# The last seven value steps as 64-row tiles in two PSUM banks, two of them set between score pairs

## The chip, the core and the metric

The kernel runs on one core of one Trainium2 chip. The metric is device time in microseconds (us), the median of repeated runs. Before the change it is 1230.41 us (three runs, 1230.26 to 1230.48). Durations and waits come from one profiled execution of the kernel before; its span from first to last instruction is 1229.5 us.

## The reference: attention with one key head, a gated FFN, and a gate that mixes them

```python
def _A_ref(x, wq, wk, wv, wo):                    # S = 2048, D = 512, H = 32, Dh = 16
    q = (x @ wq).reshape(B, S, H, Dh).transpose(0, 2, 1, 3)
    k = x @ wk                                    # one key and one value head for all 32
    v = x @ wv
    scores = einsum("bhqd,bkd->bhqk", q, k) * (Dh ** -0.5)
    p = softmax(scores, axis=-1)
    o = einsum("bhqk,bkd->bhqd", p, v)
    return o.transpose(0, 2, 1, 3).reshape(B, S, H * Dh) @ wo

def _B_ref(x, w_gate, w_up, w_down):              # F = 1376
    return (gelu(x @ w_gate) * (x @ w_up)) @ w_down

g = sigmoid((x * gate_w).sum(-1, keepdims=True))
return g * _A_ref(x, ...) + (1 - g) * _B_ref(x, ...)
```

All inputs are 32-bit floats.

## The kernel before

**The two kinds of attention step.** Scores are made transposed, keys on the partitions. One *score pair* (S in the plan, `scores`, line 745) is two matmuls of 51 rows by 128 columns over 512 queries, one per head, one in the lower and one in the upper 64 rows of TensorE's array. They fill a tile `s` of 128x1024 (two PSUM banks), and ScalarE takes one exponential over it into `p` (line 749). A *value visit* (V in the plan, `pv`, line 816) multiplies the `p` of four heads by the values: four matmuls of 128 rows (128 keys) by 32 columns, head j writing partitions 32j to 32j+31 of `acc`, one PSUM bank. Data is plain 32-bit there, and each such matmul appears in the trace as two, so a visit is eight. Two score pairs feed one visit. A unit `u` is four heads by 512 queries over 16 key chunks, so 16 visits; there are 32 units and 512 visits.

**The FFN in between.** Gate, up and down projections run as pairs of matmuls `z` and `y` (`pair_mm`, line 515), each 64 rows by 128 columns, in the two row halves of the array at once. `z` lies in one of the three `s` tiles, `y` in the bank of pool `ps_f`. PSUM has eight banks: three `s` tiles of two, one for `acc` (`ps_a`), one for `y` (`ps_f`).

**What sets the order.** The table `PLAN` is the order of TensorE's work written out by hand, one line for each FFN job, with letters that `play` carries out: H starts a job, F is one pair of its matmuls, R ends it and puts its evictions on VectorE, S is a score pair, Z a score pair into the third `s` tile, V2 is two visits. Engines work their own queues in that order. The last line is the last down projection, and then the last seven visits (505 to 511) with the last four score pairs.

**What comes after the last visit.** `norm(31)` is the last normalisation: on VectorE, in two halves of 256 columns, it forms the denominators (`zsum`, line 776) and numerators (`nsum`, line 779) straight from `acc`, then line 773 (a shuffle), 782 (reciprocals), 785 (the product), 790 and 794 (the split in a high and a low part, `oh` and `ol`). For the other units `acc` is copied to a tile `n1` first. Meanwhile TensorE makes the output projection of the last 512 queries, 36 matmuls for three of four head blocks in the tiles `wos` (three) and `wof` (in `ps_f`), and then 12 matmuls with the block that `norm` has just finished; VectorE adds each of the four results to `acc` of the FFN (line 627), and SP's queue writes it out (line 628).

Of the kernel before, what the change touches and what calls it, by code (L numbers as in the profile page):

```python
# [9 lines left out]
F32 = mybir.dt.float32  # L10
# [9 lines left out]
P = 128  # L20
S = 2048
D = 512
H = 32
DH = 16
F = 1376
TG = 512
NTG = S // TG
NC = D // P
NKC = S // P
# [12 lines left out]
EVERY = 3  # L42
PB = 12
STAGE = 4
PLAN = [
# [62 lines left out]
]  # L108


# [1 line left out]
def mix_kernel(ctx, tc, xT, wq, wo, wf, out):  # L112
    nc = tc.nc
# [4 lines left out]
    ps_f = ctx.enter_context(tc.tile_pool(name="ps_f", bufs=1, space=PSUM))  # L118
# [73 lines left out]
    vt = pp.tile([P, TG], F32, name="vt")  # L192
# [122 lines left out]
    def source(kind, n, c):  # L315
        if kind == "x":
            return xT[n, :, c]
        if kind == "o":
            return wo[:, c]
        t = 2 if kind == "d" else c  # L320
        return wf[(chunks[n][1] - 1) % NF][:, t * D : (t + 1) * D]
# [23 lines left out]
    def fetch():  # L345
        while supply and len(raw) < STAGE - 1:
            p = supply.pop(0)
            t = cp.tile([P, D], F32, tag="st", name="st", bufs=STAGE)
            nc.sync.dma_start(t, source(*p))
            raw.append((p, t))  # L350
# [86 lines left out]
    for ti, tg in enumerate(order):  # L437
        xh, xl = xs[tg]
        last = ti == NTG - 1
# [55 lines left out]
    def flush(q):  # L495
        while q:
            q.pop(0)()
# [144 lines left out]
    def ffn_jobs():  # L642
        for n, (tg, r) in enumerate(chunks):
            if r and n > 1:
                yield gate_job(n)
            if r == 5 or r == NF - 1:
                flush(chain)
                batch = hold[:]
                hold.clear()
                if r == NF - 1 and tg + 1 < NTG:  # L650
                    reload_h(tg + 1)
                for i in (0, 2):
                    yield down_job(batch, i)

    def wo_jobs():
        for g in range(NTG - 1):
            for i in (0, 2):
                yield wo_job(g, i)

    nsteps = 8 * NTG * NKC  # L660
# [24 lines left out]
    with tc.If(v > 0):  # L685
        with tc.tile_pool(name="gp", bufs=1) as gp:
# [4 lines left out]
            with tc.For_i(0, NTG * NB, 1) as gb:  # L691
                with tc.For_i(0, 2, 1) as a:
# [4 lines left out]
                    for i in range(4):  # L697
                        for h in range(4):
                            rs = slice(64 * (h % 2), 64 * (h % 2) + KR)
# [27 lines left out]
    pb = {}  # L727
    accp = {}
# [22 lines left out]
    def norm(u):  # L751
        g, ub = divmod(u, 8)
        b, a = divmod(ub, 2)
        ac = accp.pop(u)
        new = lambda tag: mp.tile([P, TG], F32, tag=tag, name=f"{tag}{u}", bufs=1)
        if a == 0:
            flush(bg)
            c0, tz = new("n0"), new("nz")
            nc.vector.tensor_copy(c0, ac)
            bg.append(lambda: nc.vector.tensor_scalar(tz, c0, mkb, None, op0=ALU.mult))  # L760
            bg.append(lambda: nc.vector.tensor_scalar(c0, c0, mk, None, op0=ALU.mult))
            at[g, b] = c0, tz
            return
        N, z = at.pop((g, b))
        last = u == 8 * NTG - 1
        r = new("n1")
        c1 = ac
        if not last:
            c1 = r
            nc.vector.tensor_copy(c1, ac)  # L770

        def shuffle(cs):
            nc.vector.stream_shuffle(r[:, cs], z[:, cs], [(i + 16) % 32 for i in range(32)])

        def zsum(cs):
            nc.vector.scalar_tensor_tensor(z[:, cs], c1[:, cs], mk, z[:, cs], op0=ALU.mult, op1=ALU.add)

        def nsum(cs):
            nc.vector.scalar_tensor_tensor(N[:, cs], c1[:, cs], mkb, N[:, cs], op0=ALU.mult, op1=ALU.add)

        def recip(cs):
            nc.vector.reciprocal(z[:, cs], r[:, cs])

        def scale(cs):
            nc.vector.tensor_mul(N[:, cs], N[:, cs], z[:, cs])

        def high(cs):
            if (g, b) not in O:
                O[g, b] = [mp.tile([P, TG], F32R, tag=t, name=f"{t}{u}", bufs=4) for t in ("oh", "ol")]
            nc.vector.tensor_copy(O[g, b][0][:, cs], N[:, cs])  # L790

        def low(cs):
            oh, ol = O[g, b]
            nc.vector.tensor_sub(ol[:, cs], N[:, cs], oh[:, cs])

        if last:
            flush(bg)
            for cs in (slice(0, 256), slice(256, 512)):
                for fn in (zsum, nsum, shuffle, recip, scale, high, low):
                    fn(cs)  # L800
            return
        full = slice(0, TG)
        for fn in (zsum, nsum, shuffle):
            bg.append(lambda fn=fn: fn(full))
        for i in range(4):
            bg.append(lambda i=i: recip(slice(i * P, (i + 1) * P)))
        for fn in (scale, high, low):
            bg.append(lambda fn=fn: fn(full))

    def pv(s):  # L810
        u, kc = divmod(s, NKC)
        if kc == 0:
            accp[u] = ps_a.tile([P, TG], F32, tag="pa", name=f"acc{u}")
        vt = (v1, v2)[u % 2]
        for j in range(4):
            nc.tensor.matmul(accp[u][32 * j : 32 * j + 32], vt[:, kc], pb[s][:, j // 2, (j % 2) * TG : (j % 2 + 1) * TG],  # L816
                             start=(kc == 0), stop=(kc == NKC - 1), skip_group_check=True)
        del pb[s]

    at_s, at_v = [0], [0]  # L820
# [5 lines left out]
    def visit(k):  # L826
        flush(chain if at_v[0] == 0 else [])
        for _ in range(k):
            assert 2 * at_v[0] + 1 < at_s[0]
            pv(at_v[0])  # L830
            at_v[0] += 1
            if at_v[0] % NKC == 0 and at_v[0] < nsteps:
                norm(at_v[0] // NKC - 1)
# [37 lines left out]
    queues = {"f": ffn_jobs(), "w": wo_jobs()}  # L871
    for line in PLAN:
        kind, word = line.split(":")
# [4 lines left out]
    now[0] += 16  # L878
    run_later()
    norm(8 * NTG - 1)  # L880

    g = NTG - 1
# [49 lines left out]
```

## Time and profile before

| | |
|---|---|
| median of the runs | 1230.41 us (1230.26 to 1230.48) |
| profiled execution, first to last instruction | 1229.5 us |
| PE busy | 1222.6 us (99%) |
| ACT busy | 1029.4 us (84%) |
| DVE busy | 546.1 us (44%) |
| POOL busy | 216.9 us (18%) |
| granted TensorE clock, mean | 0.999 |

The runs' median lies 0.9 us above the profiled span. PE is TensorE's matmuls, PEld its weight loads, DVE is VectorE, ACT ScalarE, POOL GpSimd. A busy PE counts from a matmul's start to its modelled end, and matmuls overlap; so how fast PE goes is read from the distance of starts. In a row of the timeline the first two numbers are the start and the stretch that the merged instructions cover, and the bracket at the end is the idle time before them on that engine, and what ended it.

### The profile page before, as it was taken

To read this page: it belongs to the slowest core of one execution; us is meant where nothing else is said; L and a number is where in the kernel's file an instruction comes from. 1 tells how busy PE (TensorE), PEld (TensorE's weight loads), DVE (VectorE), ACT (ScalarE), POOL (GpSimd) and SP (SyncE) were. 2 spreads that over 40 slices of the span, in tenths; PEclk is the share of its full clock that TensorE was granted. 3 is DMA by queue.
4 is the path that set the end of the run, shared out by engine and by line. 5 is a ranking of instruction groups with operands and counts; after the bars stand their busy time and mean duration, and the time that the engine had idled before them with its cause. 6 is when DMAs were issued, how large, how long until landed. Compare 5 with 4: busy or idle time off the path is not lost.

```text
span 1229.5 us, 23232 instructions
## 1 busy us (share of the span) xinstructions
PE 1222.6 (99%) x9742; PEld 671.4 (55%) x9742; DVE 546.1 (44%) x812; ACT 1029.4 (84%) x1127; POOL 216.9 (18%) x188
## 2 busy tenths in 40 slices
PE   9999999999999999999999999999999999999998
PEld 6875455555554555455555555654554555545545
DVE  7774422656245151545436152263626244044624
ACT  5549888888888888998888888889888898889983
POOL 5422201222121010212112020121311011012100
PEclk9999999999999999999999999999999999999999
DMA  8641202212021110122211120111211211002000
GB/s 333 211 135 52 72 1 58 66 53 79 27 68 51 44 32 23 49 57 67 66 35 58 39 76 15 42 44 56 83 41 49 75 49 32 23 27 66 15 1 35
DMA packets 39835, 73.88 MB, mean 60 GB/s; under 512 B 5488, under 2 KB 5744, under 8 KB 39728
## 3 DMA queue, kind: packets, MB, share of 16 engines
q1 hardware_dynamic: 39184, 71.32, 18.9%
q8 instruction: 77, 1.26, 0.4%
q0 software_dynamic: 256, 0.79, 0.2%
q14 instruction: 30, 0.25, 0.1%
q10 hardware_dynamic: 288, 0.26, 0.1%
HBM read 57.41 MB, written 14.94 MB: 59 GB/s over the span
## 4 chain that ended last, share of the span: by engine, by line
PE 93%; DVE 0%; ACT 0%; issue 0%
PE acc L816 38%; PE s L745 23%; PE z L515 21%; PE y L515 10%; PE wos L501 1%; PE u L501 0%; DVE acc L627 0%; ACT p L749 0%; PE wof L501 0%; DVE sq L545 0%; DVE sq L544 0%; DVE gs L541 0%; ACT sq L548 0%
## 5 line engine op out<-in xcount | busy, mean ns | idle before, releaser
L749 ACT ACTIVATE p<-s 128x1024 f32<-128x1024 f32 x1024 | 976.3, 1026 | 139.1 <-PE s L745 136.2
L816 PE MATMUL acc<-p,v 128*32 128x512 f32 x4096 | 484.8, 597 | 0.0
L745 PE MATMUL s<-Q,kp 51*128 51x512 f32 x2048 | 384.8, 415 | 0.1
L745 PEld LDWEIGHTS s<-Q,kp 51*128 51x128 f32 x2048 | 184.2, 184 | 214.1 <-ACT p L749 124.0
L816 PEld LDWEIGHTS acc<-p,v 128*32 128x32 f32 x4096 | 114.3, 109 | 250.8 <-issue 242.1
L187 POOL TENSOR_TENSOR gl<-st,gh 128x512 fp32r<-128x512 f32 x80 | 114.0, 1444 | 754.3 <-PE s L745 375.5
L515 PE MATMUL z<-xh,gh 64*128 64x512 f32 x312 | 125.9, 403 | 0.0
L515 PE MATMUL y<-xh,gh 64*128 64x512 f32 x312 | 125.8, 403 | 0.0
L515 PE MATMUL y<-xl,gh 64*128 64x512 f32 x312 | 122.4, 392 | 0.0
L515 PE MATMUL z<-xl,gh 64*128 64x512 f32 x312 | 122.1, 391 | 0.0
L515 PE MATMUL z<-xh,gl 64*128 64x512 f32 x312 | 121.8, 390 | 0.0
L515 PE MATMUL y<-xh,gl 64*128 64x512 f32 x312 | 121.7, 390 | 0.0
L541 DVE COPY gs<-z 128x512 f32<-128x512 f32 x39 | 27.0, 692 | 195.3 <-PE y L515 128.5
L187 POOL TENSOR_TENSOR dl<-st,dh 128x512 fp32r<-128x512 f32 x44 | 57.3, 1304 | 127.8 <-PE s L745 94.0
L515 PE MATMUL z<-dh,hh 64*128 64x512 f32 x176 | 69.5, 395 | 0.0
L515 PE MATMUL y<-dh,hh 64*128 64x512 f32 x176 | 69.5, 395 | 0.0
L515 PE MATMUL y<-dl,hh 64*128 64x512 f32 x176 | 68.9, 392 | 0.0
L515 PE MATMUL z<-dl,hh 64*128 64x512 f32 x176 | 68.8, 391 | 0.0
L515 PE MATMUL z<-dh,hl 64*128 64x512 f32 x176 | 68.8, 391 | 0.0
L515 PE MATMUL y<-dh,hl 64*128 64x512 f32 x176 | 68.7, 391 | 0.0
L515 PEld LDWEIGHTS z<-xh,gh 64*128 64x128 f32 x312 | 58.0, 186 | 15.6 <-POOLq L523 7.3
L515 PEld LDWEIGHTS z<-xl,gh 64*128 64x128 f32 x312 | 58.3, 187 | 8.2
(173 smaller groups left out, 1458.0 us busy)
## 6 DMA issues: line engine op xcount, KB each, us to landing
st<-wf SPq DMA_DIRECT2D x125, 256.0 KB
scr<-q SPq DMA_DIRECT2D x16, 512.0 KB
Q<-scr SPq DMA_DIRECT2D x64, 128.0 KB
Q<-scr SPq DMA_DIRECT2D x64, 64.0 KB
out<-acc SPq DMA_DIRECT2D x16, 256.0 KB
xr<-xT SPq DMA_DIRECT2D x6, 512.0 KB
st<-xT SPq DMA_DIRECT2D x12, 256.0 KB
xr<-xT SPq DMA_DIRECT2D x4, 256.0 KB
```

The source lines that it names most:

```text
L187: eng_l.tensor_sub(lo, src, hi)
L501: nc.tensor.matmul(ps, a, b, start=(first and q == 0), stop=(last and q == len(terms) - 1), skip_group_check=True)
L515: mm = nc.tensor.matmul(ps, a[rs], b[rs], start=(half == 0 and q == 0), stop=(half == 1 and q == len(X) - 1), skip_group_check=True)
L541: nc.vector.tensor_copy(gs, g)
L745: nc.tensor.matmul(ps[:, j * TG : (j + 1) * TG], kp[rs, kc * P : (kc + 1) * P], Q[u][rs, pr], start=True, stop=True)
L749: nc.scalar.activation(pb[s][:, pr], ps, AF.Exp, bias=0.0, scale=SCALE)
L816: nc.tensor.matmul(accp[u][32 * j : 32 * j + 32], vt[:, kc], pb[s][:, j // 2, (j % 2) * TG : (j % 2 + 1) * TG], start=(kc == 0), stop=(kc ...
```

## The change

The last seven visits are each eight matmuls in place of four: the 128 keys are split in two halves of 64 rows, and the tile is 64 rows by 32 columns. The lower half adds on to `acc`; the upper half goes to a second PSUM bank, `accb`, which begins with the first of the seven. `accb` is taken from the pool `ps_f`, the bank in which `y` of the last down projection lies. The last normalisation first copies `acc` to a tile in SBUF, adds `accb` to it, and goes on from that tile. In the last line of the plan the seven visits stand as one, one and five, not as two and five.

```diff
+HALVES = 7
 PLAN = [
...
-    "f: H F S F5 S F3 S F6 S2 F6 S F3 S F3 S F3 R S V2 S2 Z V5",
+    "f: H F S F5 S F3 S F6 S2 F6 S F3 S F3 S F3 R S V S V S Z V5",
 ]
...
         r = new("n1")
-        c1 = ac
-        if not last:
-            c1 = r
-            nc.vector.tensor_copy(c1, ac)
+        c1 = r
+        nc.vector.tensor_copy(r, ac)
...
         if last:
             flush(bg)
+            nc.vector.tensor_add(r, r, accp.pop((u, 1)))
             for cs in (slice(0, 256), slice(256, 512)):
                 for fn in (zsum, nsum, shuffle, recip, scale, high, low):
                     fn(cs)
...
         vt = (v1, v2)[u % 2]
+        by_halves = nsteps - s <= HALVES
+        if nsteps - s == HALVES:
+            accp[u, 1] = ps_f.tile([P, TG], F32, tag="pf", name="accb")
         for j in range(4):
-            nc.tensor.matmul(accp[u][32 * j : 32 * j + 32], vt[:, kc], pb[s][:, j // 2, (j % 2) * TG : (j % 2 + 1) * TG],
-                             start=(kc == 0), stop=(kc == NKC - 1), skip_group_check=True)
+            cols = slice(32 * j, 32 * j + 32)
+            w = pb[s][:, j // 2, (j % 2) * TG : (j % 2 + 1) * TG]
+            if by_halves:
+                for r, ac in ((0, accp[u]), (64, accp[u, 1])):
+                    rs = slice(r, r + 64)
+                    nc.tensor.matmul(ac[cols], vt[rs, kc], w[rs], start=(r > 0 and nsteps - s == HALVES),
+                                     stop=(kc == NKC - 1), skip_group_check=True)
+            else:
+                nc.tensor.matmul(accp[u][cols], vt[:, kc], w, start=(kc == 0), stop=(kc == NKC - 1), skip_group_check=True)
         del pb[s]
```

First, TensorE's order at the last visits, from the score pair after the last FFN matmul to the five visits at the end, before (`Q`, `kp` are the queries and keys, `v_76` the values; a wait names the engine that is waited for):

```order
L745 MATMUL s<-Q_12177,kp 128x512 [waits Activation_49]
L745 MATMUL s<-Q_12177,kp 128x512
L816 MATMUL acc_12577<-p,v_76 32x512 x8
L745 MATMUL s<-Q_12177,kp 128x512 [waits Activation_49]
L745 MATMUL s<-Q_12177,kp 128x512
L745 MATMUL s<-Q_12177,kp 128x512 [waits Activation_49]
L745 MATMUL s<-Q_12177,kp 128x512
L745 MATMUL s<-Q_12177,kp 128x512 [waits DVE_49]
L745 MATMUL s<-Q_12177,kp 128x512
L816 MATMUL acc_12577<-p,v_76 32x512 x14
```

The same place in the change, its first score pair, first visit and the pair behind it:

```order
L746 MATMUL s<-Q_12177,kp 128x512 [waits Activation_49]
L746 MATMUL s<-Q_12177,kp 128x512
L824 MATMUL acc_12577<-p,v_76 32x512
L824 MATMUL accb<-p,v_76 32x512 [waits DVE_49]
L824 MATMUL acc_12577<-p,v_76 32x512
L824 MATMUL accb<-p,v_76 32x512
L824 MATMUL acc_12577<-p,v_76 32x512
L824 MATMUL accb<-p,v_76 32x512
L824 MATMUL acc_12577<-p,v_76 32x512
L824 MATMUL accb<-p,v_76 32x512
L746 MATMUL s<-Q_12177,kp 128x512 [waits Activation_49]
L746 MATMUL s<-Q_12177,kp 128x512
```

A score pair has moved up between the first and the second visit, and the second matmul of the first visit waits for VectorE, which no visit there did before.

Second, VectorE's order from the last evictions of the down projection to the first steps of the last normalisation, before:

```order
L617 SCALAR_TENSOR_TENSOR acc_11092<-y,gc,acc_11092 128x512 [waits PE_49]
L776 SCALAR_TENSOR_TENSOR nz_12513<-acc_12577,mk,nz_12513 128x256 [waits PE_49]
L779 SCALAR_TENSOR_TENSOR n_12512<-acc_12577,mkb,n_12512 128x256 [waits DVE_49]
L773 STREAM_SHUFFLE n_12851<-nz_12513 128x256 [waits DVE_49]
L782 RECIPROCAL nz_12513<-n_12851 128x256 [waits DVE_49]
```

And in the change:

```order
L618 SCALAR_TENSOR_TENSOR acc_11092<-y,gc,acc_11092 128x512 [waits PE_49]
L769 COPY n_12880<-acc_12577 128x512 [waits PE_49]
L797 TENSOR_TENSOR n_12880<-n_12880,accb 128x512 [waits DVE_49,PE_49]
L775 SCALAR_TENSOR_TENSOR nz_12513<-n_12880,mk,nz_12513 128x256 [waits DVE_49]
L778 SCALAR_TENSOR_TENSOR n_12512<-n_12880,mkb,n_12512 128x256
L772 STREAM_SHUFFLE n_12880<-nz_12513 128x256 [waits DVE_49]
L781 RECIPROCAL nz_12513<-n_12880 128x256 [waits DVE_49]
```

Two instructions over all 512 columns stand ahead of the first half; everything behind them has kept its order. Elsewhere no engine's order differs.

## The prediction

> **What bounds the kernel now.** I read the page's busy times first, then the chain of waits, then the timeline of the last 25 us, where everything that is changed lies.
>
> ```profile
> PE 1222.6 (99%) x9742; PEld 671.4 (55%) x9742; DVE 546.1 (44%) x812; ACT 1029.4 (84%) x1127; POOL 216.9 (18%) x188
> PE 93%; DVE 0%; ACT 0%; issue 0%
> ```
>
> TensorE sets the end: 93% of the chain is PE. So a change costs what it adds to PE's path, plus what it adds behind PE's last matmul. The chain in order of time, near its end:
>
> ```profile
> 1189.98 2.71 PE acc L816 x24
> 1192.70 0.89 PE s L745 x6
> 1193.59 3.57 PE acc L816 x32
> 1197.16 0.43 PE s L745 x2
> ...
> 1205.48 0.23 PE s L745 x2
> ...
> 1206.40 0.24 PE s L745 x2
> 1206.64 1.85 PE acc L816 x16
> 1208.49 0.89 PE s L745 x6
> 1209.39 4.43 PE acc L816 x40
> 1213.82 6.34 PE wos L501 x27
> 1220.16 2.04 PE wof L501 x9
> 1222.20 0.69 PE wos L501 x3
> 1222.90 0.02 issue
> 1222.92 2.79 DVE acc L627 x4
> ```
>
> Prices come out of these rows. Three visits take 2.71 us and four 3.57, so one visit is 0.86 and a run of visits has 0.13 on top (2.71 - 3 x 0.86). A score pair among FFN matmuls takes 0.23 (1205.48), but behind visits 0.43 (1197.16), and three there take 0.89 = 3 x 0.23 + 0.20. So going from scores to visits and back costs 0.13 + 0.20 = 0.33 us, and VectorE's four last additions (2.79) are the only thing of weight behind PE.
>
> **The change part by part.** *The work on PE.* The seven visits are still seven by 0.86 us if the eight tiles of a visit run at once, as its four do now and as z and y do. The trace has no tile of 64 rows by 32 columns. At the other end, the two row halves take turns and a visit takes 2 x 0.86. I take 0.86: 32-column tiles overlap in every visit (eight matmuls in one 0.86), and the row halves overlap in the FFN. Starts of neighbouring tiles lie 7 ns apart (below: four loads cover 0.13 us at 109 ns each), so four more tiles add 0.03 at the end of each run of visits, 0.09 for three runs.
>
> *The wait on the second bank.* This is the largest term, and these rows of the timeline carry it:
>
> ```profile
> 1206.44 0.75 DVE L617 SCALAR_TENSOR_TENSOR acc<-z,gc,acc 128x512 f32<-128x512 f32 x1 [17.13 <-PE z L515]
> 1206.57 1.92 PE L816 MATMUL acc<-p,v 128*32 128x512 f32 x16
> 1207.03 0.13 PEld L816 LDWEIGHTS acc<-p,v 128*32 128x32 f32 x4 [0.30 <-issue]
> 1207.11 0.74 DVE L617 SCALAR_TENSOR_TENSOR acc<-y,gc,acc 128x512 f32<-128x512 f32 x1
> L816 PEld LDWEIGHTS acc<-p,v 128*32 128x32 f32 x4096 | 114.3, 109 | 250.8 <-issue 242.1
> ```
>
> accb takes the bank of y, and y is read last, at 1207.11 + 0.74 = 1207.85. Before, the first visit starts at 1206.57. In the change only its very first matmul (to acc) can go then; the second, to accb, waits until 1207.85 and about 0.05 more for the signal (estimate: the last wof matmul ends at 1224.53 + 0.39, VectorE starts at 1224.96). TensorE's queue is in order, so the rest of the visit, the score pair behind it and all the later visits stand behind that matmul: 1207.90 - 1206.57 = **1.33 us**. Bounds: nothing, if the first visit came later anyway; 1.33 + 0.86, if the first matmul's work, done meanwhile, had to be followed by a full visit more. I take 1.33, since the other seven matmuls still need a visit's length.
>
> *The plan.* Before, the end is two visits, three pairs, five visits: 1.85 + 0.89 + 4.43 = 7.17. Now it is one, one, one, two, five: 0.99 + 0.43 + 0.99 + 0.66 + 4.43 = 7.50, one round trip more, **+0.33**. This holds only if going from 64x128 tiles to 64x32 costs what going to 128x32 costs. Lower bound: both now have 64 rows, and no crossing costs anything. The nearest rows are the crossing from visits to the projection, where the rows stay 128 and only the columns change, beside a change of data type alone in the prologue:
>
> ```profile
> 1213.75 0.50 PE L501 MATMUL wos<-woh,oh 128*128 128x512 f32 x1
> 1214.09 0.40 PE L501 MATMUL wos<-wol,oh 128*128 128x512 f32 x1
> 1214.32 0.39 PE L501 MATMUL wos<-woh,ol 128*128 128x512 f32 x1
> ...
> 76.63 0.40 PE L501 MATMUL g<-xh,gl 128*128 128x512 f32 x1
> 76.63 0.59 PEld L260 LDWEIGHTS pv<-ident,vt 128*128 128x128 f32 x4
> 76.86 0.60 PE L260 MATMUL pv<-ident,vt 128*128 128x128 f32 x4
> ```
>
> The five visits of 4.43 hold the 0.13 ahead of wos too, and its second matmul comes after 0.34, not 0.23. A crossing where only columns change costs as much as one where both change. The data type is not the reason: at 76.63 the weight load for the other type starts with the matmul before it, and the next matmul follows after 0.23. So I take the full price.
>
> The Trainium skill, page "TensorEngine Tiling (Array Packing)", section "Tiling Modes", says that changing the tiling mode, not just the tile, drains TensorE, and lists 64x128 and 64x32 as two modes. By that rule the round trip is paid; without it the visits would cross for nothing. No run here shows 64x32.
>
> ScalarE stays hidden:
>
> ```profile
> 1208.97 1.94 ACT L749 ACTIVATE p<-s 128x1024 f32<-128x1024 f32 x2 [1.20 <-PE s L745]
> ```
>
> It idles 1.20 us there. An exponential is 0.97 and starts some 0.5 after its pair. With the pairs at about 1208.9, 1210.4 and 1210.7, the last ends near 1212.9; the visit that needs it starts near 1214.5. Without that cover the five visits would wait for it.
>
> *The last normalisation.* Two instructions over 512 columns stand ahead of it, a copy out of PSUM and an addition with one operand in PSUM:
>
> ```profile
> 1151.31 0.69 DVE L541 COPY gs<-z 128x512 f32<-128x512 f32 x1 [2.31 <-PE z L515]
> 1152.03 0.69 DVE L544 SCALAR_TENSOR_TENSOR sq<-gs 128x512 f32<-128x512 f32 x1
> L281 DVE TENSOR_TENSOR q<-pq,q x16: 677/681/692, 18.6 to 72.2; 128x512 fp32r<-128x512 f32 x16
> ...
> 1217.73 0.43 DVE L794 TENSOR_TENSOR ol<-n,oh 128x256 fp32r<-128x256 f32 x1
> 1218.08 0.48 DVE L776 SCALAR_TENSOR_TENSOR nz<-acc,mk,nz 128x256 f32<-128x256 f32 x1
> ...
> 1221.92 0.43 DVE L794 TENSOR_TENSOR ol<-n,oh 128x256 fp32r<-128x256 f32 x1
> 1222.92 2.11 DVE L627 SCALAR_TENSOR_TENSOR acc<-wos,gt,acc 128x512 f32<-128x512 f32 x3 [0.57 <-PE wos L501]
> 1223.18 0.19 PEld L501 LDWEIGHTS wos<-woh,oh 128*128 128x128 f32 x1
> ```
>
> From a copy to what uses it is 0.72 (1151.31 to 1152.03); an addition with PSUM takes 0.68 and the same 0.03 behind it. Together 1.44 us later. TensorE hardly feels it: the third tile needs the second half at 1223.18, which is ready at 1222.35 for the low part that is loaded 0.45 later still, so about 1.2 of 1.44 is covered and PE slips by 0.2. VectorE feels it: after its last split at 1221.92 it could go on 0.35 later (as 1217.73 to 1218.08), at 1222.27, and starts line 627 at 1222.92. That cover is 0.65, so its four additions come 1.44 - 0.65 = 0.79 later, and they then follow each other at about 0.67, not 0.68, which gives back some 0.03. **+0.76**, VectorE being the last in place of PE; SP's four writes (line 628) follow each addition and move with it. Bounds: 0.2 (only TensorE's slip counts) and 1.44 (no cover).
>
> **Sum:** 1.33 + 0.33 + 0.09 + 0.76 = 2.51 us, all in the last 25 us. The profiled span of 1229.5 becomes 1232.0; the runs' median lies 0.9 above the span, so **1232.9 us**.
>
> **The rivals.** *The crossings between 64-row tiles are free.* For it: both tiles split the rows in the same way, and scores and FFN, both 64x128, cross freely at 0.23. Against it: the wos rows. It saves what the sum has for crossings behind the first: 2 x 0.20 and 2 x 0.11 (0.13 less the stagger of the first pass), about 0.6: 1232.3.
>
> *The row halves take turns.* Each of seven visits takes 1.72: 7 x 0.86 = 6.0 more, 1238.9. For it: nothing in the trace shows rows and columns split at once. Against it: each split alone overlaps. It decides as soon as a visit takes over 0.9.
>
> The Trainium skill, page "TensorE: Matmul & The Clock Gate", part 3, gives 16 tiles of 32x32 a measured speedup of 10.6 and about 4 ns for each tile, by which eight tiles would run at once. No run here shows such tiles.
>
> *The wait for accb costs little*, because VectorE's release comes earlier or the pairs behind make the time up. Then 1231.6. Against it: the order rows, where that matmul waits for VectorE, and VectorE's two evictions are back to back.
>
> *VectorE's masked sums slow down*, since they now read SBUF alone:
>
> ```profile
> L776 DVE SCALAR_TENSOR_TENSOR nz<-n,mk,nz x15: 752/1783/1791, 153.5 to 1143.5; 128x512 f32<-128x512 f32 x15
> 1213.75:1224.60 10.85, 0.00 (x0) 1.00 0.00 1
> ```
>
> Out of SBUF they took 1.78 at the median but 0.75 at best, each over 512 columns. If the slow price held, four by half of 1.03 add 2.1: 1235.0. Against it: the second row is POOL's busy time in the tail, none; the 0.75 then needs an idle POOL, which is my reading of the spread, not shown.
>
> *Faster than before* needs free crossings, no wait and a covered tail at once, and gains under 1 us even then (before, all crossings there are 0.6).
>
> **How the numbers follow.** Forecast 0.55, free crossings 0.18, taking turns 0.10, little wait 0.09, slow sums 0.04, faster for a reason that I don't see 0.04. What this kernel's runs can tell from no change is 0.2%, 2.46 us. The forecast of 2.51 lies on that line, so it is halved: 0.28 slower, 0.27 the same. Slower is 0.28 + 0.10 + 0.04 = 0.42; the same is 0.27 + 0.18 + 0.09 = 0.54; faster 0.04. The range leaves out the turns above and the odd case below. It reaches down to 1231.2 (little wait, and a covered tail in part) and up to 1235.0 (slow sums, or a second pass that is not quite hidden in three runs of visits, 3 x 0.43).
>
> **What would show it.** In the profile after: the first visit's load for accb at about 1207.9, with VectorE's line 618 as what ended its wait; score pairs between visits of 0.43 in the chain, visits of 0.86 in the run of five (it would begin near 1211.0); wos at about 1215.5, 1.75 later than before; the four additions at the end starting at about 1225.5, with no idle time before them. It is wrong if the loads between score pairs and visits start with the matmul before them, if a run of five visits takes clearly more than 4.5 us, or if accb's first matmul does not wait.

## The result, and the profile after

The changed kernel takes 1233.05 us (median of 11 runs, 1232.83 to 1233.16), the kernel before, beside it, 1230.13 (11 runs, 1229.91 to 1231.27). The ratio is 1.0023, with a 95% interval of 1.0014 to 1.0032: 2.9 us slower. The profiled execution of the changed kernel spans 1231.4 us, only 1.9 more than that of before. Most of the rest lies in the first 82 us, which the change does not touch; ScalarE's rows there, of before and after, each read from its own timeline:

```profile
81.32 1.03 ACT L749 ACTIVATE p<-s 128x1024 f32<-128x1024 f32 x1 [5.51 <-PE s L745]
```

```profile
80.42 1.03 ACT L750 ACTIVATE p<-s 128x1024 f32<-128x1024 f32 x1 [5.64 <-PE s L746]
```

The same instruction comes 0.90 us later in the profile of before. In each of the nine later profiles the run's own time lies 1.75 to 1.83 us above the span, so with its span of 1229.5 the profiled execution of before was one of about 1231.3 (an estimate from these), as long as the slowest of its 11 runs; the 0.9 us that stands in the prediction between span and median is not a fixed distance. So a span cannot be compared with a span here to better than about 1 us. I compare two distances inside the tail instead. *A* goes from the start of the last score pair that follows an FFN matmul to the start of the first `wos` matmul; it is TensorE's part. *B* goes from there to the start of VectorE's last addition; it is the part behind. In the timeline of before they are 1213.75 - 1206.24 = 7.51 and 1224.96 - 1213.75 = 11.21 (the `wos` row stands in the prediction):

```profile
1206.24 0.40 PE L745 MATMUL s<-Q,kp 51*128 51x512 f32 x2
...
1224.96 0.75 DVE L627 SCALAR_TENSOR_TENSOR acc<-wof,gt,acc 128x512 f32<-128x512 f32 x1
```

The same rows of the changed kernel, and between them what happens at the first visit:

```profile
1205.27 0.40 PE L746 MATMUL s<-Q,kp 51*128 51x512 f32 x2
1205.47 0.75 DVE L618 SCALAR_TENSOR_TENSOR acc<-z,gc,acc 128x512 f32<-128x512 f32 x1 [17.13 <-PE z L516]
...
1205.60 1.04 PE L824 MATMUL acc<-p,v 64*32 64x512 f32 x2
...
1206.14 0.74 DVE L618 SCALAR_TENSOR_TENSOR acc<-y,gc,acc 128x512 f32<-128x512 f32 x1
1206.93 0.10 PEld L824 LDWEIGHTS accb<-p,v 64*32 64x32 f32 x1 [1.20 <-DVE acc L618]
...
1214.52 0.50 PE L502 MATMUL wos<-woh,oh 128*128 128x512 f32 x1
...
1224.83 2.06 DVE L628 SCALAR_TENSOR_TENSOR acc<-wos,gt,acc 128x512 f32<-128x512 f32 x3
...
1226.80 0.74 DVE L628 SCALAR_TENSOR_TENSOR acc<-wof,gt,acc 128x512 f32<-128x512 f32 x1
```

A is now 9.25 (+1.74), B is 12.28 (+1.07); together +2.81, close to the 2.92 of the medians. The first visit's first matmul goes at 1205.60, and the load of its second stands until VectorE has read `y` (1206.14 + 0.74) and 0.05 longer. The chain of waits of the changed kernel shows where TensorE stops being the bound (pieces of 0.05 us and less are left out, but for one that is needed below):

```profile
1205.48 1.41 DVE acc L618 x2
1206.94 0.61 PE accb L824
1207.59 0.39 PE accb L824 x2
1208.02 0.44 PE s L746 x2
1208.46 0.54 PE acc L824
...
1209.48 0.66 PE s L746 x4
1210.14 0.54 PE acc L824
1210.73 0.38 PE acc L824
1211.16 0.38 PE acc L824
...
1214.70 0.68 DVE n L769
...
1215.41 0.02 DVEq L797
...
1215.48 0.70 DVE n L797
...
1224.91 1.98 DVE acc L628 x3
```

VectorE's two evictions are on the chain ahead of the visits, and everything behind the last visit is VectorE, where before it was `wos`, `wof` and only then four additions. The run of five goes on in steps of 0.43 (1210.73, 1211.16), two to a visit of eight tiles.

### The profile page after: what moved, and what is told of

Its sections match the earlier page's. It is cut to its first block, busy times and chain, and to the rows that moved or that the text cites. A ratio compares the mean times of both kernels' runs of the same rounds, so it can differ in the third digit from the quotient of the medians.

```text
span 1231.4 us, 23347 instructions
## 1 busy us (share of the span) xinstructions
PE 1224.1 (99%) x9798; PEld 671.5 (55%) x9798; DVE 546.4 (44%) x814; ACT 1029.4 (84%) x1127; POOL 217.2 (18%) x188
## 4 chain that ended last, share of the span: by engine, by line
PE 92%; DVE 1%; ACT 0%; DVEq 0%; issue 0%
PE acc L827 37%; PE s L746 23%; PE z L516 21%; PE y L516 10%; PE acc L824 0%; DVE nz L781 0%; PE u L502 0%; ACT p L750 0%; DVE acc L628 0%; PE accb L824 0%; DVE acc L618 0%; DVE n L772 0%; DVE nz L775 0%; DVE n L784 0%; DVE ol L793 0%; DVE n L778 0%
## 5 line engine op out<-in xcount | busy, mean ns | idle before, releaser
L827 PE MATMUL acc<-p,v 128*32 128x512 f32 x4040 | 478.4, 597 | 0.0
```

The costliest lines, as they stand in the source:

```text
L827: nc.tensor.matmul(accp[u][cols], vt[:, kc], w, start=(kc == 0), stop=(kc == NKC - 1), skip_group_check=True)
```

## The experiments

The theory is the sum of the prediction with its one visible miss put right: a wait of 1.33 us on TensorE for `y`, 0.33 for one more round trip between scores and visits, 0.03 of stagger for each run of visits by halves (four tiles more, their starts 7 ns apart), and VectorE's tail, now 1.07. The main rivals are that the wait is only passed on, that round trips are dear only with 64-row tiles, and that VectorE's longer tail is hidden.

The differences are fractions of a microsecond, and the interval of each ratio is about 0.1% (1.2 us) to either side. So each verdict rests on A and B, and the medians stand beside them as a second reading. A and B come from one execution of each kernel, but where an edit leaves a stretch alone they repeat: A is 9.25 in the change and 9.24 in e3, 7.51 before and in e8; B is 11.21 before and in e7 and 11.25 in e1. Differences of B up to about 0.05 therefore say nothing.

| kernel | A, us | B, us | A + B against before (18.72) | median against before, timed beside it | ratio, 95% interval |
|---|---|---|---|---|---|
| the change | 9.25 | 12.28 | +2.81 | +2.92 | 1.0023 (1.0014 to 1.0032) |
| e1, plan only | 7.85 | 11.25 | +0.38 | +0.35 | 1.0003 (0.9993 to 1.0012) |
| e2, first visit whole | 7.90 | 12.28 | +1.46 | +1.46 | 1.0011 (1.0001 to 1.0021) |
| e3, sum in its own tile | 9.24 | 12.05 | +2.57 | +2.65 | 1.0021 (1.0012 to 1.0031) |
| e4, y read first | 8.60 | 12.28 | +2.16 | +2.21 | 1.0019 (1.0009 to 1.0029) |
| e5, five halves, old plan | 7.53 | 12.29 | +1.10 | +1.19 | 1.0008 (0.9998 to 1.0017) |
| e6, e5 mended | 7.53 | 12.00 | +0.81 | +0.93 | 1.0008 (0.9998 to 1.0017) |
| e7, two more trips | 8.18 | 11.21 | +0.67 | +0.68 | 1.0006 (0.9996 to 1.0015) |
| e8, copy only | 7.51 | 11.24 | +0.03 | +0.12 | 1.0000 (0.9991 to 1.0010) |

e1 to e4 were timed beside a kernel before of 1230.21 us, e5 to e8 beside one of 1230.31.

**e1: the new order of the plan alone.**

```diff
-    "f: H F S F5 S F3 S F6 S2 F6 S F3 S F3 S F3 R S V2 S2 Z V5",
+    "f: H F S F5 S F3 S F6 S2 F6 S F3 S F3 S F3 R S V S V S Z V5",
```

> The kernel before with the new order of its last plan line only: visits one, one, five, all of 128 rows, no second bank, no copy. Theory (a round trip from scores to visits and back costs 0.33 us whatever the rows): from the last score pair among the FFN matmuls to wos 7.51 + 0.33 = 7.84 us, time 1230.13 + 0.33 = 1230.5. Rival (a round trip is only dear with tiles of 64 rows, and what the change lost there came with them): 7.5 us, time unchanged. Rival (ScalarE can no longer hide): a gap before a score pair or ahead of the five visits, over 8.2 us.

A is 1214.14 - 1206.29 = 7.85, 0.34 more than before. The chain of waits of this kernel, to be held against the one of the changed kernel above:

```profile
1206.69 0.99 PE acc L816 x8
1207.69 0.43 PE s L745 x2
1208.12 0.99 PE acc L816 x8
1209.11 0.66 PE s L745 x4
1209.78 4.43 PE acc L816 x40
```

A pair alone between visits takes 0.43 here and 0.44 there, two pairs 0.66 and 0.66. So the crossing costs the same whether the visit's tiles have 128 rows or 64, and the rival that 64-row tiles cross otherwise, cheaper or dearer, falls. So does the prediction's rival of free crossings, by which a pair would take 0.23 there. ScalarE did not show: no gap stands in that chain.

**e7: two round trips more, all visits whole.**

```diff
-    "f: H F S F5 S F3 S F6 S2 F6 S F3 S F3 S F3 R S V2 S2 Z V5",
+    "f: H F S F5 S F3 S F6 S2 F6 S F3 S F3 S F3 R S V S V S V Z V4",
```

> The kernel before with its last plan line as one, one, one and four visits with a score pair ahead of each: two round trips more than before, all visits whole. Theory (each round trip costs 0.33 us): from the last score pair among the FFN matmuls to wos 7.51 + 0.67 = 8.18 us, time 1230.15 + 0.67 = 1230.8. Rival (a pair this close behind the one ahead has to wait for ScalarE): a gap on TensorE that ends with ScalarE, 8.5 us or more.

In the timeline of this kernel:

```profile
1205.20 0.40 PE L745 MATMUL s<-Q,kp 51*128 51x512 f32 x2
...
1213.38 0.50 PE L501 MATMUL wos<-woh,oh 128*128 128x512 f32 x1
```

A is 8.18, so 0.67 for two: the price is 0.33 each and adds up. The chain of this kernel has no gap that ends with ScalarE, so that rival falls, and keeps VectorE's four additions of 2.79 behind TensorE, as before.

**e2: the second bank is needed one visit later.**

```diff
-HALVES = 7
+HALVES = 6
```

> The changed kernel, but the first of the seven visits stays whole (128 rows, acc alone), so that the second bank is first needed one round trip later. Theory (1.33 us of the change is TensorE standing until VectorE has read y): no wait of any visit for VectorE, from the last score pair to wos 9.25 - 1.33 = 7.92 us, time 1233.05 - 1.33 = 1231.7. Rival (the wait is only passed on, to a score pair that then waits for its exponential): 8.9 us or more, time 1232.7 or more.

The timeline of this kernel, weight loads of the first and second visits:

```profile
1205.67 0.16 PEld L827 LDWEIGHTS acc<-p,v 128*32 128x32 f32 x8 [0.37 <-issue]
1206.66 0.19 PEld L746 LDWEIGHTS s<-Q,kp 51*128 51x128 f32 x2 [0.84 <-ACT p L750]
1207.10 0.10 PEld L824 LDWEIGHTS acc<-p,v 64*32 64x32 f32 x1 [0.25 <-issue]
1207.10 0.10 PEld L824 LDWEIGHTS accb<-p,v 64*32 64x32 f32 x1
```

The load for `accb` follows that for `acc` at once: VectorE has read `y` by 1206.94, 0.16 earlier. A is 1213.24 - 1205.34 = 7.90: 1.35 has gone, 1.33 for the wait and the rest for the stagger of one run of halves less, and nothing took its place. The 0.84 in front of the score pair is not a new wait; the loads of a visit end well ahead of its matmuls, and in the timeline of before the same 0.84 stands behind the first two visits:

```profile
1208.42 0.53 PEld L745 LDWEIGHTS s<-Q,kp 51*128 51x128 f32 x6 [0.84 <-ACT p L749]
```

**e4: VectorE reads y first.**

```diff
-            for k, ps in ((i, z), (i + 1, y)):
+            order = ((i, z), (i + 1, y))
+            if tg == NTG - 1 and i == 2 and r > 0:
+                order = order[::-1]
+            for k, ps in order:
```

> The changed kernel, but VectorE reads y before z after the last down projection. Theory (the second matmul of the first visit waits for the read of y alone): it starts 0.75 + 0.05 us after VectorE's first eviction starts, 0.67 after the visit's first matmul instead of 1.33, from the last score pair to wos 9.25 - 0.66 = 8.59 us, time 1232.4. Rival (it waits until both evictions are done): 9.25 and 1233.05 as before this edit.

The timeline of this kernel (its lines stand 3 lower than the changed kernel's):

```profile
1206.38 0.75 DVE L621 SCALAR_TENSOR_TENSOR acc<-y,gc,acc 128x512 f32<-128x512 f32 x1 [17.14 <-PE y L516]
...
1207.18 0.10 PEld L827 LDWEIGHTS accb<-p,v 64*32 64x32 f32 x1 [0.55 <-DVE acc L621]
```

The load comes 1207.18 - 1206.38 = 0.80 after the start of that one eviction, while the second, of `z`, is still running; A is 1214.77 - 1206.17 = 8.60. So it is the bank of `y` that is waited for, and nothing else that VectorE does there. Counted from the visit's first matmul (1206.50 here), two evictions ahead of it cost 1.33, one costs 0.68.

**e3: the sum in a tile of its own.** In the changed kernel the sum of `acc` and `accb` lies in the tile `r`, into which the shuffle then writes.

```diff
-        c1 = r
-        nc.vector.tensor_copy(r, ac)
+        c1 = cp.tile([P, TG], F32, tag="gs", name="nc", bufs=1) if last else r
+        nc.vector.tensor_copy(c1, ac)
...
-            nc.vector.tensor_add(r, r, accp.pop((u, 1)))
+            nc.vector.tensor_add(c1, c1, accp.pop((u, 1)))
```

> The changed kernel, but the sum of acc and accb lies in a tile of its own, not in the one that the shuffle writes. Theory (the shuffle starts 0.12 us later in each half because it overwrites what the numerators have just read, and has to wait for them to end): numerators to shuffle 0.40 us again, not 0.52, from wos to the last addition 12.28 - 0.24 = 12.04 us, time 1232.8. Rival (sums out of SBUF end later than sums out of PSUM, whatever the shuffle writes): still 0.52 and 12.28, time 1233.05.

Numerators and shuffle of the first half, in the timeline of the changed kernel:

```profile
1216.60 0.48 DVE L778 SCALAR_TENSOR_TENSOR n<-n,mkb,n 128x256 f32<-128x256 f32 x1
...
1217.12 0.44 DVE L772 STREAM_SHUFFLE n<-nz 128x256 f32<-128x256 f32 x1
```

and in that of e3:

```profile
1216.58 0.48 DVE L778 SCALAR_TENSOR_TENSOR n<-nc,mkb,n 128x256 f32<-128x256 f32 x1
...
1216.99 0.44 DVE L772 STREAM_SHUFFLE n<-nz 128x256 f32<-128x256 f32 x1
```

0.52 against 0.41. In the changed kernel the shuffle starts after the numerators have ended (1216.60 + 0.48 = 1217.08); with a tile of its own it starts before they end, as the same two do in the kernel before (1214.29 and 1214.69). B falls by 0.23, two halves of it.

**e5: five visits by halves and the old plan.** No wait, no extra trip; what is left is the tail.

```diff
-HALVES = 7
+HALVES = 5
...
-    "f: H F S F5 S F3 S F6 S2 F6 S F3 S F3 S F3 R S V S V S Z V5",
+    "f: H F S F5 S F3 S F6 S2 F6 S F3 S F3 S F3 R S V2 S2 Z V5",
```

> The changed kernel with the old last line of the plan, and only the last five visits by halves: no wait for y, no extra round trip, the last normalisation as in the change. Theory (what is left is VectorE's longer way to the end): no wait, from the last score pair among the FFN matmuls to wos 7.51 + 0.03 = 7.54 us, from wos to the last addition 12.28 as in the change, against 11.21 before, so time 1230.15 + 0.03 + 1.07 = 1231.25. Rival (only TensorE's slip of 0.2 counts): wos to the last addition 11.4, time 1230.4.

The rows of its timeline from which A and B come:

```profile
1205.12 0.40 PE L746 MATMUL s<-Q,kp 51*128 51x512 f32 x2
...
1212.65 0.50 PE L502 MATMUL wos<-woh,oh 128*128 128x512 f32 x1
...
1224.94 0.74 DVE L628 SCALAR_TENSOR_TENSOR acc<-wof,gt,acc 128x512 f32<-128x512 f32 x1
```

A is 7.53 and B 12.29. The tail's loss, 1.08, is there without the wait and without the extra trip, and the rival in which only TensorE's slip counts (11.4) falls.

**e8: the kernel before with one copy more.** Nothing but a copy of `acc` ahead of the last normalisation, which goes on from the copy.

```diff
-        c1 = ac
-        if not last:
-            c1 = r
-            nc.vector.tensor_copy(c1, ac)
+        c1 = cp.tile([P, TG], F32, tag="gs", name="nc", bufs=1) if last else r
+        nc.vector.tensor_copy(c1, ac)
```

> The kernel before, whose last normalisation first copies acc to a tile of its own and goes on from that: one more instruction of 512 columns on VectorE, nothing else. Theory (behind its last split VectorE has 0.65 us of cover before TensorE's first finished tile): its last split ends 0.72 us later, the four additions begin 0.07 later, wos to the last addition 11.21 + 0.07 = 11.28 at most, time 1230.2. Rival (no cover, all of VectorE's time counts): 11.9, time 1230.9. Rival (sums out of SBUF are slow): 0.5 us more for each of the four masked sums, wos to the last addition over 13.

VectorE in the timeline of this kernel:

```profile
1212.95 0.69 DVE L768 COPY nc<-acc 128x512 f32<-128x512 f32 x1 [6.05 <-PE acc L814]
1213.68 0.48 DVE L774 SCALAR_TENSOR_TENSOR nz<-nc,mk,nz 128x256 f32<-128x256 f32 x1
...
1221.73 0.43 DVE L792 TENSOR_TENSOR ol<-n,oh 128x256 fp32r<-128x256 f32 x1
1222.07 2.06 DVE L627 SCALAR_TENSOR_TENSOR acc<-wos,gt,acc 128x512 f32<-128x512 f32 x3
1224.05 0.74 DVE L627 SCALAR_TENSOR_TENSOR acc<-wof,gt,acc 128x512 f32<-128x512 f32 x1
```

The first `wos` matmul starts at 1212.81. Counted from there, the copy makes everything up to the split 0.73 to 0.75 later, yet the four additions begin only 0.09 later, and B is 1224.05 - 1212.81 = 11.24, 0.03 more than before. The cover of 0.65 is real, and it is just used up: VectorE no longer waits ahead of the additions (1222.07 is 0.34 after the split, as between any two such instructions). The masked sums out of SBUF take 0.48, exactly as out of PSUM, so the rival of slow sums falls.

**e6: e5 with both small losses of VectorE mended.** The sum gets its own tile, and `accb`, which TensorE finishes last, is copied first and `acc` added to it.

```diff
-        c1 = r
-        nc.vector.tensor_copy(r, ac)
+        c1 = cp.tile([P, TG], F32, tag="gs", name="nc", bufs=1) if last else r
+        nc.vector.tensor_copy(c1, accp.pop((u, 1)) if last else ac)
...
-            nc.vector.tensor_add(r, r, accp.pop((u, 1)))
+            nc.vector.tensor_add(c1, c1, ac)
```

> As the kernel with the old plan line and five visits by halves, and with the sum in a tile of its own, made by copying accb and adding acc. Theory: numerators to shuffle 0.40 us in both halves (0.24 less), copy to addition 0.72 and not 0.80 (the addition no longer has to wait for two engines), from wos to the last addition 12.28 - 0.24 - 0.07 = 11.97, time 1230.95. Rival (the 0.07 is the tile form or the place of acc, not a second wait): copy to addition stays 0.80, time 1231.0.

From copy to addition, in the timeline of the changed kernel:

```profile
1214.68 0.69 DVE L769 COPY n<-acc 128x512 f32<-128x512 f32 x1 [7.80 <-PE accb L824]
1215.48 0.69 DVE L797 TENSOR_TENSOR n<-n,accb 128x512 f32<-128x512 f32 x1
```

and in that of e6:

```profile
1212.94 0.69 DVE L769 COPY nc<-accb 128x512 f32<-128x512 f32 x1 [6.10 <-PE accb L824]
1213.67 0.69 DVE L797 TENSOR_TENSOR nc<-nc,acc 128x512 f32<-128x512 f32 x1
```

0.80 against 0.73. In the change that addition waits for two engines, VectorE's own copy and TensorE's last matmul to `accb`, although TensorE has finished well before; where the copy has done the waiting for TensorE, the addition is 0.07 earlier. The changed kernel's chain above has a row between the two for the second wait (1215.41, DVEq, VectorE's instruction queue); the chain of e6 has none. The tile is not the reason: in e3 the sum has a tile of its own, the row is there, and the addition still comes 0.80 behind the copy (1214.66 and 1215.46). That the addition reads `acc` in e6 and `accb` in the others was not varied alone. B is 1224.76 - 1212.76 = 12.00 (11.97 expected). This is the cheapest form found in which visits run by halves, and it is still 0.8 us behind the kernel before on the trace.

## Why the prediction was right, and where it was off

**The wait on the second bank: right, place and size.** Predicted 1.33, with the load 0.05 after the eviction of `y`; measured 1206.93 - 1205.60 = 1.33. e2 takes 1.35 out by needing the bank later, and e4 halves it, to 0.68, by reading that bank first. The rival of a wait that costs little falls with both.

**The extra round trip: right.** Predicted 0.33; 0.34 in e1 and 0.67 for two in e7, both with 128-row tiles. With halves it is 7.90 - 7.53 = 0.37 between e2 and e5, of which 0.03 is the stagger of a second run of halves. The prediction took the full price from the crossing into the projection, where only the columns change; the price held for the crossing to 64x32, which that row did not show. The Trainium skill, page "TensorEngine Tiling (Array Packing)", section "Tiling Modes", says that changing the mode drains TensorE, with 64x32 a mode of its own; the trace agrees, 0.43 for a lone pair behind 128x32 tiles and 0.44 behind 64x32.

**Eight tiles at once: right.** Two steps of 0.43 to a visit, not four; the rival of row halves that take turns, 6 us, falls with the run of five. The stagger was put at 0.09 for three runs of visits; A leaves 1.74 - 1.33 - 0.33 = 0.08.

**VectorE's tail: right in mechanism, mis-sized.** The step "together 1.44 us later" less a cover of 0.65, for 0.76, measured 1.07. The cover was right (e8). TensorE slips by 0.33 and not 0.2 (the third `wos` tile's last block starts 9.98 behind the first `wos` matmul, 9.65 before), but its last matmul ends at 1226.17, ahead of VectorE's last addition at 1226.80, so this adds nothing. What the step missed are two dependencies that the edit brought along. The addition waits for two engines, 0.07 more (e6). And since the sum lies in the tile that the shuffle overwrites, the shuffle waits in each half for the numerators to end, 0.23 together (e3). With 1.44 - 0.65, and 0.07 that the four additions gave back (from the first to the last 1.97, before 2.04), this makes 1.02 of the 1.07; the remaining 0.05 is no more than B scatters. VectorE's order as listed with the change showed both: two engines in the addition's wait, and one tile, `n_12880`, read by the sums and written by the shuffle. I counted the added instructions and did not look at what they wait for, nor at which tile they share with the ones that stay.

**The sum.** 2.51 was forecast, 2.81 lies in the trace, and the medians differ by 2.92. The time of 1232.9 came within 0.2 of 1233.05 partly by luck: it started from 1230.41, and the kernel before took 1230.13 beside the changed one, which made up for 0.28 of the 0.41 by which the forecast difference fell short of 2.92. What is left between 2.81 and 2.92 is below what these runs tell. Whether the change is slower by 0.2% stays undecided, as forecast: that bound lies inside the interval of the ratio.

**What stays open.** No run varied the masked sums that take 1.78 us elsewhere in the program. The trace of before bears out the prediction's reading of them, that the fast ones need an idle POOL: of the fifteen at line 776 over 512 columns, POOL is idle beside the two of 0.75 (at 153.50 and 1074.85), and busy with line 187 beside the other thirteen. One of each kind, with POOL's work beside the slow one:

```profile
153.50 0.75 DVE L776 SCALAR_TENSOR_TENSOR nz<-n,mk,nz 128x512 f32<-128x512 f32 x1
...
223.36 3.05 POOL L187 TENSOR_TENSOR gl<-st,gh 128x512 fp32r<-128x512 f32 x2 [13.46 <-PE s L745]
...
223.48 1.78 DVE L776 SCALAR_TENSOR_TENSOR nz<-n,mk,nz 128x512 f32<-128x512 f32 x1
```

In the tail, where POOL is idle, the source, PSUM or SBUF, makes no difference.

## What to carry to other kernels

Before a tile takes a bank over from another tile, find the last reader of that bank and the moment it ends: on an engine that works in order, one matmul that waits there holds everything behind it, and to need the bank one step later (e2) costs nothing, if it is free by then; here it was, by 0.16 us. Count how often TensorE goes back and forth between tile shapes: here 0.33 us for each round trip between scores and visits, and the same within 0.04 whether the visits are whole or by halves. When an edit puts data into an existing tile, list who else writes that tile; the new order of reads and writes costs time even on one engine, here 0.23 us.

## What the runs showed of the hardware that was not expected

An instruction of VectorE that needs nothing of the one ahead of it starts before that one ends: the shuffle of e3 0.41 us behind the start of numerators of 0.48. One that reads what the one ahead writes starts after its end (the addition of e6 0.73 behind a copy of 0.69), and so does one that only overwrites what the one ahead reads (the shuffle of the change, 0.52 behind numerators of 0.48). A wait for a second engine cost 0.07 us even where that engine had finished well before. And two profiled executions of the same first part of a program can lie 0.97 us apart when they reach the tail (1206.24 and 1205.27), 0.90 of it from the first 82 us, so that differences of this size are read from distances within a trace.
